# Loads, first stage and evictions of batch 1 moved in a Fourier filter with a snake feed-forward layer

## The chip, the cores and the metric

The kernel runs on one core of a Trainium2 chip. The metric is the device time of one execution in microseconds (us); the median of three runs counts.

## The reference

The input `x` has 8 batches of 3008 positions with 256 channels. Each batch is filtered in the frequency domain, and every position then goes through a feed-forward layer of width 2048 with the snake activation:

```python
X = np.fft.rfft(x, axis=1)
y = np.fft.irfft(X * (filt_r + 1j * filt_i)[None], n=3008, axis=1)
h = y.reshape(24064, 256) @ w_in            # w_in 256 x 2048
s = np.sin(alpha * h)
out = (h + s * s / (alpha + 1e-9)) @ w_out  # w_out 2048 x 256
```

## The kernel before

**The arithmetic.** The transform of 3008 = 47 x 64 points is done as matrix products in fp16. Each batch passes four stages: `first` (DFT over 47, 16 matmuls `pa` of 512 columns, each evicted as half precision into `t1_h`), `forward` (DFT over 64 with the twiddles in `d_t`, 12 pairs of matmuls `pb`), the product with the filter, `inverse` (12 pairs `pc` with `e_t`) and `last` (16 groups `pd`, evicted into `y`). Between `first` and `forward`, and between `inverse` and `last`, the data goes through DRAM to change its layout: SP stores `t1_h` into `d1` (L186), GpSimd's queue loads it back as `t2` (L193); SP stores `g` into `d2` (L239) and loads `t4` from it (L244). The filter is applied by `product` (L215, p = xf x real part) and `cross` (L221, L222: the halves of `xf` swapped by two SP copies `xs`, times `f_t[1]`, added to p). Both run on VectorE. Because the swap needs a sign, one half of `f_t[1]` is negated once, in two instructions of 64 x 3072 (`negate`, L602), before batch 1's cross products. Batch 0 goes another way, without DRAM, by VectorE transposes (L413) at the start of the kernel; it uses the filter without that sign.

**The feed-forward layer.** The 2048 x 256 hidden layer runs in chunks of 512 positions. `hidden(k, jb)` makes one of 16 tiles of a chunk: two matmuls into a `ph` buffer (L540), a cosine on ScalarE (L544), and `v = cos - 1 - ph` on VectorE (L545). `project` multiplies the `v` of the chunk before by `w_out` (groups of eight matmuls `po`, L557); ScalarE copies the result to `o` (L565), and SP stores it. `w_in` is scaled by alpha and `w_out` by -0.5/alpha on GpSimd (`weights_in`, L482, six pieces; `weights_out`, L514, three pieces of four blocks; the last four blocks on ScalarE, L512).

**Buffers.** PSUM has four `ph` buffers (`h`), two for `po` (`o`), and two (`f`) that all transform matmuls share. `evac` (L160, L162) empties an `f` buffer: every third call goes to VectorE, the others to ScalarE, unless the call names the engine.

**The order of the work.** Engines take their instructions in program order, and program order is written by hand. At the start stand batch 0's stages; then GpSimd gets the weight products and the loads of batch 1's `x`. The main loop counts steps: each makes two `hidden` tiles and one or two `project` groups (chunk 0 has only the tiles), and `slot(step)`, called twice a step, takes from a sorted list what is due. The list is filled by `put(time, function, ...)`; of the entries marked `pe`, one is taken per call, and more only when they are overdue by a step. For batch 1 `first` is due from 7.9, `load_t2` at 12.5, `negate` at 13 and 14, `forward` from 17.5, `cross` from 21.5, `inverse` from 23.5.

**Order of loads.** SP loads `w_in` in six pieces, then `w_out` in two. `after(ins, other)` makes a DMA wait for another to land: the first piece of `w_in` waits for the last quarter of the filter (`marks["filt", 1, 1]`), and each `x` load of batch 1 for the first half of `w_out`. The filter comes in quarters on GpSimd's queue, real and imaginary part of each half of `s`; `other_half` copies each quarter to the other 64 partitions.

Of the kernel before, what the change touches and what calls it, by code (L numbers as in the profile page):

```python
# [62 lines left out]
def kernel(  # L63
# [10 lines left out]
    nc = tc.nc  # L74
# [12 lines left out]
    def after(ins, other):  # L87

        tc.add_manual_dep(ins.ins, other.ins.name, mybir.DependencyInfo(
            mybir.DependencyClass.Sync, mybir.DependencyReason.DATA), reason="order of loads")  # L90
# [43 lines left out]
    f_t = [filt_t[:, k] for k in range(2)]  # L134

    marks = {}
# [20 lines left out]
    def evac(dst, src, on_act=None):  # L157
        flip[0] = (flip[0] + 1) % 3
        if flip[0] if on_act is None else on_act:
            marks["act"] = nc.scalar.copy(out=dst, in_=src)  # L160
        else:
            marks["dve"] = nc.vector.tensor_copy(out=dst, in_=src)  # L162

    class Spectral:
# [59 lines left out]
        def inverse(self, w):  # L224
            b = self.b
            pr = self.p.pop(w)
            if w % 3 == 0:
                self.g = gpool.tile([128, 6, C], FP16, name=f"g_{b}_{w}", tag="g")
            ps = fps.tile([128, 2, C], FP32, name=f"pc_{b}_{w}", tag="f")
            for i in range(2):  # L230
                for k, pt in enumerate(pr):
                    nc.tensor.matmul(out=ps[:, i, :], lhsT=e_t[:, 2 * w + i, :],  # L232
                                     rhs=pt[:, i, :], start=(k == 0), stop=(k == len(pr) - 1))
            i0 = 2 * (w % 3)
            evac(self.g[:, i0:i0 + 2, :], ps)
            if w % 3 == 2:
                for p in range(2):
                    a0 = p * NS + 6 * (w // 3)
                    nc.sync.dma_start(out=self.d2[a0:a0 + 6, :, :].rearrange("s n c -> n s c"),  # L239
                                      in_=self.g[64 * p:64 * p + 64, :, :])  # L240
# [46 lines left out]
    def spread_alpha(i):  # L287

        ps = hps.tile([128, 4, 128], FP32, name=f"al_bc_{i}", tag="h")
        for a in range(4):  # L290
            for k, part in enumerate(parts):
                nc.tensor.matmul(out=ps[:, a, :], lhsT=one[:, 4 * i + a:4 * i + a + 1].to_broadcast([128, 128]),
                                 rhs=part, start=(k == 0), stop=(k == 2))
        nc.scalar.copy(out=alpha[:, i // 2, 512 * (i % 2):512 * (i % 2) + 512], in_=ps.rearrange("p a b -> p (a b)"))

    for g in range(2):
        gs = slice(12 * g, 12 * g + 12)
        for k, filt in enumerate((filt_r, filt_i)):
            for q in range(2):
                if (g, k, q) == (0, 1, 1):  # L300
                    split_alpha()
                off, step = ((12 * g) * C, C) if q == 0 else ((N1 - 12 * g) * C, -C)
                marks["filt", g, k] = nc.gpsimd.dma_start(
                    out=f_t[k][64 * k + 32 * q:64 * k + 32 * q + 32, gs, :],
# [91 lines left out]
    for i in range(16):  # L396
        own, tag = (fps, "f") if i % 3 == 2 else (hps, "h")
        ps = own.tile([128, 512], FP32, name=f"pa_0_{i}", tag=tag)
# [64 lines left out]
    for g in range(6):  # L463
        own, tag = (t2pool, "t2") if g < 3 else (gpool, "g")
        j0 = 1024 * (g // 3) + 384 * (g % 3)
        js = slice(j0, j0 + (256 if g % 3 == 2 else 384))
        w_in32.append((js, own.tile([128, 2, js.stop - js.start], FP32, name=f"w_in_{g}", tag=tag)))
        ins = nc.sync.dma_start(out=w_in32[g][1], in_=w_in_v[:, :, js])
        if g == 0:
            after(ins, marks["filt", 1, 1])  # L470
    nc.sync.dma_start(out=wf_t, in_=wf_dram.ap())
    nc.sync.dma_start(out=wi_t, in_=wi_dram.ap())
    w_out32 = vpool.tile([128, 16, C], FP32, name="w_out32", tag="v")
    for jb in range(0, 16, 8):
        ins = nc.sync.dma_start(out=w_out32[:, jb:jb + 8],
                                in_=moe_w_out[128 * jb:128 * jb + 1024].rearrange("(b p) c -> p b c", p=128))
        marks.setdefault("w_out", ins)
    s1 = Spectral(1)
# [37 lines left out]

    spread_alpha(2)
    spread_alpha(3)
    for step in ([(weights_in, g) for g in range(6)] + [(s1.load_x, 0), (weights_out, 0), (s1.load_x, 1),
                 (weights_out, 4), (s1.load_x, 2), (weights_out, 8), (s1.load_x, 3)]):  # L520
        step[0](*step[1:])
    warm_pe(12)
    last_0(0, 4)
# [69 lines left out]
    def put(at, fn, *args, pe=False):  # L593
        pending.append((at, len(pending), pe, fn, args))
# [4 lines left out]
    def negate(i):  # L599

        gs = slice(12 * i, 12 * i + 12)
        nc.vector.tensor_scalar(out=f_t[1][0:64, gs, :], in0=f_t[1][0:64, gs, :],  # L602
                                scalar1=-1.0, scalar2=None, op0=ALU.mult)

    for i in range(2):
        put(13 + i, negate, i)
    for n0, n, at in ((6, 5, 1.5), (11, 4, 12.5), (15, 4, 14), (19, 4, 15.5), (23, 4, 17), (27, 5, 19)):
        put(at, last_0, n0, n, fps, "f", True)
    for b in range(1, B):
        s = s1 if b == 1 else Spectral(b)  # L610
        z = 48 * b
        if b > 1:
            for ch in range(4):
                put((22,27,32,37)[ch] if b == 2 else z - 92 + 7 * ch, s.load_x, ch)
        for i in range(16):
            put(7.9 + 0.3 * i if b == 1 else 36 + 0.66 * i if b == 2 else z - 67 + 0.66 * i, s.first, i, pe=True)
        for g in range(4):
            put(12.5 if b == 1 else max(z - 56, 46.5), s.load_t2, g)
        for u in range(12):
            inv = 23.5 + 1.25 * u if b == 1 else 59 + 2.1 * u if b == 2 else z - 40.8 + 2.3 * u  # L620
            fwd = inv - (6 if b == 1 else 6)
            put(fwd, s.forward, u, pe=True)
            put(fwd + (0.5 if b == 1 else 1.5), s.product, u)
            if s.fused:
                put(fwd + (4 if b == 1 else 4.5), s.cross, u)
            put(inv, s.inverse, u, pe=True)
        for ch in range(4):
            put(z - (9.5 if b == 1 and ch < 3 else (10.5, 10.5, 10.5, 3)[ch]), s.load_t4, ch)
        for u in range(16):
            put(z + (u - (5 if b == 1 else 6.5) if u < 4 else 2 * u - 9), s.last, u, pe=True)  # L630
# [15 lines left out]
    step = 0  # L646
# [43 lines left out]
```

## Time and profile before

| What | Value |
|---|---|
| Median of 3 runs (lowest, highest) | 789.85 us (789.4, 790.68) |
| Profiled execution, span from the first to the last instruction | 786.7 us |
| TensorE busy | 773.5 us |
| VectorE busy | 657.6 us |
| ScalarE busy | 616.5 us |
| GpSimd busy | 79.5 us |
| First hidden matmul starts | 36.79 us |
| First `pa` matmul of batch 1 starts | 47.63 us |
| Mean granted TensorE clock | 1.000 |

The profile is of one execution. PE is TensorE's matmuls, PEld its weight loads, DVE VectorE, ACT ScalarE, POOL GpSimd, SP SyncE, which here only issues DMAs. A row of a timeline gives start, duration, engine, source line, operation, tile written `<-` tile read, shape and count; in brackets stands the idle time before it and what ended that. Matmul rows overlap, since they are pipelined: what one costs is read from the distance between the starts of two.

### The profile page before, as it was taken

How to read it: one execution, taken by the hardware profiler on the slowest of the kernel's cores; microseconds unless marked ns; L12 is line 12 of the kernel's file. 1: busy time of each engine (PE TensorE's matmuls, PEld its weight loads, DVE VectorE, ACT ScalarE, POOL GpSimd, SP SyncE). 2: the span in 40 equal slices, each digit the busy share in tenths (PEclk: the TensorE clock that was granted, in tenths of full speed). 3: DMA queues.
4: the chain of work that ended last, by engine and by line, in shares of the span. 5: the costliest groups of instructions: out<-in, count | busy, mean ns of one | idle time of the engine just before them, and what ended most of it. 6: DMA issues, size and time to landing. Idle time of an engine off the chain costs nothing.

```text
span 786.7 us, 16619 instructions
## 1 busy us (share of the span) xinstructions
PE 773.5 (98%) x5799; PEld 535.0 (68%) x5799; DVE 657.6 (84%) x1172; ACT 616.5 (78%) x1208; POOL 79.5 (10%) x125
## 2 busy tenths in 40 slices
PE   8998999999999999999999999999999999999998
PEld 4756766666667766777666766777666776766666
DVE  7887997899878997799977998799987999777773
ACT  5797878888878887888877888788887887777674
POOL 6442000200020000200020000200002000000000
PEclk9999999999999999999999999999999999999999
DMA  9965568665473646554575454845556243421111
GB/s 213 258 131 157 113 145 223 153 123 133 134 198 84 134 99 195 143 120 110 120 200 128 103 106 139 224 87 113 129 155 181 61 99 81 117 62 28 41 41 54
DMA packets 87692, 100.99 MB, mean 128 GB/s; under 512 B 14488, under 2 KB 75944, under 8 KB 87608
## 3 DMA queue, kind: packets, MB, share of 16 engines
q1 hardware_dynamic: 78032, 73.73, 34.5%
q0 software_dynamic: 9360, 26.15, 17.7%
q8 instruction: 45, 0.74, 0.4%
q14 instruction: 39, 0.32, 0.1%
q10 hardware_dynamic: 216, 0.05, 0.0%
HBM read 55.72 MB, written 46.66 MB: 130 GB/s over the span
## 4 chain that ended last, share of the span: by engine, by line
PE 89%; DVE 5%; ACT 2%; DMA 2%; issue 1%; SPq 1%; ACTq 0%; DVEq 0%
PE po L557 39%; PE ph L540 38%; PE pa L181 3%; PE pd L254 2%; DVE v L545 2%; PE pb L201 2%; PE pc L232 2%; DMA xs<-xf 1%; ACT cos_all L544 1%; DMA al<-in_moe_alpha_dram 1%; PE warm L381 1%; PE pc L453 0%; SPq L585 0%; ACT t_h L160 0%; DVE filt_t L162 0%
## 5 line engine op out<-in xcount | busy, mean ns | idle before, releaser
L545 DVE SCALAR_TENSOR_TENSOR v<-cos_all,ph 128x512 f16<-128x512 f32 (+1 forms) x768 | 483.0, 672 | 108.1 <-ACT cos_all L544 104.8
L544 ACT ACTIVATE cos_all<-ph 128x512 f32<-128x512 f32 (+1 forms) x768 | 411.1, 592 | 93.9 <-PE ph L540 92.9
L540 PE MATMUL ph<-y,w 128*128 128x512 f16 (+1 forms) x1536 | 388.4, 374 | 1.7 <-DVE y L162 0.9
L557 PE MATMUL po<-w,v 128*128 128x256 f16 x3008 | 389.5, 272 | 0.0
L557 PEld LDWEIGHTS <-v 128*128 128x128 f16 x3008 | 288.3, 98 | 77.7 <-issue 1.4
L540 PEld LDWEIGHTS <-w 128*128 128x128 f16 x1536 | 147.9, 98 | 106.5 <-issue 6.1
L565 ACT COPY o<-po 128x512 f32<-128x512 f32 (+1 forms) x97 | 55.6, 574 | 20.2 <-PE po L557 12.9
L204 ACT CAST xf<-pb 128x512 f16<-128x512 f32 x84 | 50.0, 595 | 16.4 <-PE pb L201 12.7
L193 POOL DMA_DIRECT2D t<-d x56 | 36.4, 669 | 204.6 <-DMA out_dram<-o 99.8
L160 ACT CAST t_h<-pa 96x512 f16<-96x512 f32 x74 | 43.3, 585 | 10.6 <-PE pa L181 10.5
L141 POOL DMA_DIRECT2D x<-in_x_dram x32 | 17.1, 536 | 298.2 <-PE pc L232 171.2
L160 ACT CAST y<-pd 128x376 f16<-128x376 f32 (+1 forms) x82 | 39.5, 482 | 8.8 <-PE pd L254 5.3
L254 PEld LDWEIGHTS <-t_a 96*128 96x128 f16 x448 | 31.3, 97 | 18.7 <-issue 0.4
L181 PE MATMUL pa<-x,wf_t 94*96 94x512 f16 x112 | 42.3, 381 | 1.6 <-ACT t_h L160 1.3
L160 ACT CAST g<-pc 128x512 f16<-128x512 f32 x58 | 34.4, 593 | 8.0 <-PE pc L232 7.7
L222 DVE TENSOR_TENSOR p<-p,xs 128x512 f16<-128x512 f16 x84 | 35.7, 425 | 2.9
L254 PE MATMUL pd<-wi_t,t_a 96*128 96x94 f16 x448 | 37.1, 204 | 0.0
L221 DVE TENSOR_TENSOR xs<-xs,filt_t 128x512 f16<-128x512 f16 x84 | 35.2, 420 | 0.8 <-DMA xs<-xf 0.8
L215 DVE TENSOR_TENSOR p<-xf,filt_t 128x512 f16<-128x512 f16 x84 | 35.2, 419 | 0.0
L232 PE MATMUL pc<-p,e_t 128*128 128x256 f16 x168 | 32.1, 273 | 0.8 <-ACT xf L204 0.5
L201 PE MATMUL pb<-t,d_t 128*128 128x256 f16 x168 | 32.1, 272 | 0.2
L162 DVE CAST y<-pd 128x376 f16<-128x376 f32 (+2 forms) x46 | 24.9, 544 | 1.5 <-PE pd L343 1.0
(66 smaller groups left out, 264.4 us busy)
## 6 DMA issues: line engine op xcount, KB each, us to landing
x<-in_x_dram POOLq DMA_DIRECT2D x30, 376.0 KB, 4.9
d<-t_h SPq DMA_DIRECT2D x28, 384.0 KB
t<-d POOLq DMA_DIRECT2D x56, 192.0 KB, 4.6
xs<-xf SPq DMA_DIRECT2D x168, 64.0 KB
d<-g SPq DMA_DIRECT2D x56, 192.0 KB
t_a<-d SPq DMA_DIRECT2D x28, 384.0 KB
out_dram<-o SPq DMA_DIRECT2D x104, 80.0 KB
w_out<-in_moe_w_out_dram SPq DMA_DIRECT2D x2, 1024.0 KB
```

Of the source, the lines that this page charges most:

```text
L160: marks["act"] = nc.scalar.copy(out=dst, in_=src)
L181: marks["pe"] = nc.tensor.matmul(out=ps[0:NK, :], lhsT=wf_t, rhs=self.x[ch][:, 2 * j:2 * j + 2, :], start=True, stop=True)
L193: nc.gpsimd.dma_start(out=self.t2[g][64 * p:64 * p + 64, :, :], in_=self.d1[a0:a0 + 6, :, :].rearrange("s n c -> n s c"))
L201: nc.tensor.matmul(out=ps[:, i, :], lhsT=d_t[:, s, :], rhs=self.t2[s // 6][:, s % 6, :], start=True, stop=True)
L204: nc.scalar.copy(out=self.xf[u], in_=ps)
L232: nc.tensor.matmul(out=ps[:, i, :], lhsT=e_t[:, 2 * w + i, :], rhs=pt[:, i, :], start=(k == 0), stop=(k == len(pr) - 1))
L254: nc.tensor.matmul(out=psv[:, i, :], rhs=wi_t, start=True, stop=True, lhsT=t4_h[ch // 2][0:NK, n0 % 16 + i, cb * 128:cb * 128 + 128])
L540: nc.tensor.matmul(out=ps[:, 0:n], lhsT=w1[:, cb, jb * 128:jb * 128 + 128], rhs=y_cols[:, cb, c0:c0 + n], start=(cb == 0), stop=(cb == 1))
L544: nc.scalar.activation(out=cs[:, 0:n], in_=ps[:, 0:n], func=AFT.Sin, bias=float(np.pi / 2))
L545: marks["snake"] = nc.vector.scalar_tensor_tensor(out=v[k][:, jb, 0:n], in0=cs[:, 0:n], scalar=-1.0, in1=ps[:, 0:n], op0=ALU.add, op1=ALU. ...
L557: nc.tensor.matmul(out=pso[k][:, t % 2, :], lhsT=v[k][:, jb, 128 * t:128 * t + 128], rhs=w2[:, jb, :], start=(jb == 0), stop=(jb == 15))
L565: nc.scalar.copy(out=o[:, i0:t % 2 + 1, :], in_=pso[k][:, i0:t % 2 + 1, :])
```

## The change

Five edits, all about the time in which batch 1's transform gets going:

1. The load of `w_in` waits for the third quarter of the filter instead of the last.
2. On GpSimd the four `x` loads of batch 1 stand between the last three `w_in` products; the three `w_out` products follow all of them. Before, all six `w_in` products came first, and the `x` loads stood between the `w_out` products.
3. Batch 1's first stage is due from step 6.9 in steps of 0.35, instead of from 7.9 in steps of 0.3.
4. The evictions of batch 1's inverse stage all go to ScalarE; before, every third went to VectorE.
5. The two negations of the filter half run on GpSimd instead of VectorE, behind the `t2` loads in its queue.

```diff
@@ inverse
-            evac(self.g[:, i0:i0 + 2, :], ps)
+            evac(self.g[:, i0:i0 + 2, :], ps, True if b == 1 else None)
@@ loads of w_in
         if g == 0:
-            after(ins, marks["filt", 1, 1])
+            after(ins, marks["filt", 1, 0])
@@ GpSimd's weight products
-    for step in ([(weights_in, g) for g in range(6)] + [(s1.load_x, 0), (weights_out, 0), (s1.load_x, 1),
-                 (weights_out, 4), (s1.load_x, 2), (weights_out, 8), (s1.load_x, 3)]):
+    for step in ([(weights_in, g) for g in range(3)] + [(s1.load_x, 0), (weights_in, 3), (s1.load_x, 1),
+                 (weights_in, 4), (s1.load_x, 2), (weights_in, 5), (s1.load_x, 3)]
+                 + [(weights_out, jb) for jb in (0, 4, 8)]):
         step[0](*step[1:])
@@ negate
-        nc.vector.tensor_scalar(out=f_t[1][0:64, gs, :], in0=f_t[1][0:64, gs, :],
+        nc.gpsimd.tensor_scalar(out=f_t[1][0:64, gs, :], in0=f_t[1][0:64, gs, :],
                                 scalar1=-1.0, scalar2=None, op0=ALU.mult)
@@ the list of the main loop
-            put(7.9 + 0.3 * i if b == 1 else 36 + 0.66 * i if b == 2 else z - 67 + 0.66 * i, s.first, i, pe=True)
+            put(6.9 + 0.35 * i if b == 1 else 36 + 0.66 * i if b == 2 else z - 67 + 0.66 * i, s.first, i, pe=True)
```

## The prediction

> **What bounds the kernel now.** I read the page's busy row first, then busy time by stage, then the timelines of TensorE, VectorE, ScalarE and GpSimd through the stages that the diff touches.
>
> ```profile
> PE 773.5 (98%) x5799; PEld 535.0 (68%) x5799; DVE 657.6 (84%) x1172; ACT 616.5 (78%) x1208; POOL 79.5 (10%) x125
> 40.00:60.00 20.00, 18.61 (x104) 10.46 (x103) 17.06 (x29) 17.80 (x37) 7.93 (x8) 1.00 0.66 129
> 60.00:80.00 20.00, 17.90 (x149) 13.99 (x148) 15.10 (x26) 14.77 (x30) 5.22 (x8) 1.00 0.57 152
> 80.00:100.00 20.00, 20.00 (x147) 14.28 (x146) 19.54 (x41) 17.08 (x33) 1.09 (x2) 1.00 0.59 121
> 100.00:120.00 20.00, 19.12 (x126) 12.09 (x125) 18.76 (x37) 15.15 (x30) 1.03 (x2) 1.00 0.64 147
> 160.00:200.00 40.00, 39.95 (x299) 27.96 (x297) 37.84 (x74) 33.59 (x66) 1.03 (x2) 1.00 0.54 121
> ```
>
> The stage rows give busy us of PE, PEld, DVE, ACT, POOL, then clock, DMA share and GB/s. From 160 us on TensorE has no idle time: every microsecond won or lost before then moves the end by as much, and nothing later can win any. The stretch from 40 to 120 us, which fills the pipeline and runs batch 1's transform, is where TensorE still waits.
>
> ```profile
> 57.10 1.04 PE L557 MATMUL po<-w,v 128*128 128x256 f16 x8
> 58.25 0.38 PE L181 MATMUL pa<-x,wf_t 94*96 94x512 f16 x1
> 59.29 0.38 PE L181 MATMUL pa<-x,wf_t 94*96 94x512 f16 x1 [0.67 <-ACT t_h L160]
> 61.46 0.38 PE L181 MATMUL pa<-x,wf_t 94*96 94x512 f16 x1
> 62.51 0.38 PE L181 MATMUL pa<-x,wf_t 94*96 94x512 f16 x1 [0.67 <-ACT t_h L160]
> 66.56 0.20 PE L343 MATMUL pd<-wi_t,t_a 128*128 128x94 f16 x1 [0.34 <-ACT y L160]
> 68.69 0.38 PE L540 MATMUL ph<-y,w 128*128 128x512 f16 x1 [0.90 <-DVE y L162]
> ```
>
> Two `pa` matmuls in a row start 0.22 apart when nothing holds them; here they start 1.04 and 1.05 apart. Of the pairs 11/12 and 14/15 the second waits for ScalarE to empty the `f` buffer that the first has just filled.
>
> ```profile
> 65.58 0.95 DVE L602 TENSOR_SCALAR filt_t<-filt_t 64x3072 f16<-64x3072 f16 x1
> 66.45 0.54 DVE L162 CAST y<-pd 128x376 f16<-128x376 f32 x1
> 66.91 1.27 DVE L545 SCALAR_TENSOR_TENSOR v<-cos_all,ph 128x512 f16<-128x512 f32 x2
> 68.10 0.54 DVE L162 CAST y<-pd 128x376 f16<-128x376 f32 x1
> 75.87 0.42 DVE L215 TENSOR_TENSOR p<-xf,filt_t 128x512 f16<-128x512 f16 x1
> 46.73 2.06 ACT L544 ACTIVATE cos_all<-ph 128x512 f32<-128x512 f32 x4
> 48.64 0.60 ACT L160 CAST t_h<-pa 96x512 f16<-96x512 f32 x1
> 12.40 0.58 POOL L307 DMA_DIRECT2D e_t<-e_tbl  x1
> 17.40 0.99 POOL L307 DMA_DIRECT2D e_t<-e_tbl  x1 [0.43 <-DMA filt_t<-in_filt_r_dram]
> 67.10 5.22 POOL L193 DMA_DIRECT2D t<-d  x8 [19.14 <-DMA d<-t_h]
> ```
>
> The negations of L602 stand ahead of evictions that TensorE needs; ScalarE runs its cosines without a gap from 46.73 to 48.64; GpSimd issues batch 1's `t` loads from 67.10 to 72.32.
>
> **Part by part.** The profiled span is 786.7 us against a median of 789.85, so 3.1 us lie around the span. Gains and losses below are differences of the span, taken off the median.
>
> *w_in's load.* The third quarter's last piece was issued at 15.16; the shortest flight of that tile's loads is 7.9, so it lands at 23.0. SP now issues `w_in` then instead of at 25.47, 2.4 earlier. It overtakes the last quarter and `e_t`'s second half on the DMA engines. VectorE's copy of the last quarter at 25.66 waits 0.2 for that landing, and from there products and transposes run nearly unbroken to the first hidden matmul at 36.79, so any delay is paid in full. In the trace the last 512-byte filter packet starts at 24.2; `w_in`'s first packet came 1.06 after its issue, thus now at 24.1. Bounds 0 and 0.9 (the longest of those first `w_in` packets, 0.88, ahead of the landing's signal); no gain, since the filter itself comes no earlier. I take 0.2 lost, near the lower end, as the packets hardly overlap.
>
> *x loads between the products.* GpSimd's first three products end at 35.4 as before. Behind them the x load waits for `w_out`'s first half, which landed at 38.33 by the landings in the trace and now at about 36.0; queued behind that wait are products 3 to 5 (1.82, 1.82, 1.28) and three `w_out` products (1.91). With 0.56 for each x issue, products 3, 4, 5 end at 38.4, 40.8, 42.6; their first readers on TensorE run at 41.26, 43.06, 45.41. `w_out`'s last product ends at 48.9, its reader runs at 50.7. So nothing, covered by 1.8 us or more. If `w_out` lands no earlier, everything is 2.3 later and some 0.5 is lost. x lands 4 to 5 us after issue, long before use.
>
> *First stage from 6.9.* The order now has `pa` 0 and 1 ahead of chunk 1, and the evictions of 10 and 13 stand ahead of VectorE's next two tiles. TensorE waits of 0.82, 0.82 (the two pairs) and 0.28 (at 58.25) were 1.92 in all. New waits: ScalarE cannot evict `pa` 0 before 47.7, so `pa` 2 starts at 48.3; by then TensorE has done two `pa` (0.43) where before it had one and half a `po` group (0.67): 0.23 lost. Following the order with pitches 0.48 (ScalarE), 0.60 (VectorE), 0.87 (eight `po`), `pa` 11 and 13 still wait 0.1 and 0.25. Net 1.92-0.23-0.35 = 1.35 won; bounds 0.7 (one pair still waits 0.82 in full) and 1.9.
>
> *Negation to GpSimd, what VectorE gets.* Two instructions of 0.95 go. The waits at 66.56 and 68.69, by start pitch 0.51 and 1.06, don't both vanish: the `y` that TensorE wants at 68.69 follows a cosine that ends at 67.0, one tile (0.60) and its own 0.54, thus 68.15 at best. Won 0.5; bounds 0.2 and 1.57. Next late is that cosine.
>
> *Negation to GpSimd, what it costs.* It is queued behind the eight `t` issues, ending 9.8 after `pa` 15 starts (72.32-62.51). No row shows this operation there. Nearest is the one-input CAST, 186 ns for 16 elements and 280 for 128, which makes 2.75 for 3072; the two-input form (1272 for 512, 1815 for 768) would make 6.7. I take 2.75, as this too has one input. Cross products (L221) now wait for GpSimd, but the first comes at 81.96: covered. Not covered is the first L215, due 12.9 after `pa` 15 (75.87-62.51, less 0.5), while the second negation runs until 15.3. Do the engines hold each other up? The `e_t` issue at 17.40 took 0.99 instead of 0.58, ending 0.12 after VectorE's SBUF copy of 17.32 to 18.27: held. The `v` rows beside GpSimd's products keep their 0.61: not held, but they read PSUM. L215 reads two SBUF tiles, so I take it as held, 2.4. Behind it stand the next `v` tiles. TensorE has four `ph` buffers; a pair is wanted back 4.2 later and its chain takes 2.2, so 2.0 is covered. Lost 0.5; bounds 0 and 8.3 (below).
>
> The Trainium skill, page "SBUF — State Buffer", section "Who interferes with whom", speaks against this edit: a VectorE instruction with two SBUF inputs and a GpSimd instruction that reads SBUF exclude each other for the whole instruction. No row here has that pair; by the rule the hold stands as taken, without it the sum would be 0.5 better. Its "GPSIMD Engine Reference", section 3.1, gives 1.03 cycles per element for simple bodies and about 1.8 for a tight loop; at the latter, an estimate is 4.6 us per negation, and the sum would turn to a loss of 1.25.
>
> *Inverse evictions.* In 80 to 120 VectorE is busiest. TensorE's waits from 100.44 to 115.8 come to 2.03 by start pitch. Three `g` casts (92.77, 101.55, 109.53), 0.60 each, leave it: 1.8. ScalarE gets 3 x 0.48 where it was idle 0.60 (before 91.73) and 1.68 (before 104.88). The wait of 0.64 at 101.30 is for an `xf` behind an `xs` copy, which SP issues behind the `d` store of `g`; that store now waits for ScalarE and may go 1 us earlier, or not. I leave it out and take 1.2 of the other 1.39; bounds 0 and 2.0.
>
> Sum: -0.2+1.35+0.5-0.5+1.2 = 2.35 won: 787.5.
>
> **Rivals.** *Slower: GpSimd's negation stops VectorE.* With d us per negation the hold is 9.8+2d-12.9, the loss 2d-5.1 after cover, against 2.85 won elsewhere; it decides from d = 4.0. At 6.7: 8.3 lost, 5.4 slower net, 795.3. For it: GpSimd's two-input rows and the held issue. Against: its one-input rows. *No hold*: the `v` rows speak for it; 2.85 won, 787.0. *Nothing measurable*: the `xs` copies, not VectorE, pace 100 to 116 (for it: ScalarE's 3.0 us of waits on them), and the early `w_in` costs 0.9: 1.35+0.5-0.5-0.9 = 0.45 won, 789.4.
>
> **How the numbers follow.** Forecast 0.42, no hold 0.17, nothing 0.15, slower rival 0.26. The range starts at 785.7, where about half of each upper bound beyond the forecast comes true as well, and ends at 791.7, the slower rival with d = 4.9; beyond lie long negations. A measurement of this kernel tells about 0.2% (1.6 us) from nothing; a little of the forecast's own spread falls inside. Faster 0.57, same 0.17, slower 0.26.
>
> **What would show it.** Right: `pa` pairs without 0.67 gaps and `pa` 15 near 61.3; `ph` at 68.69 some 1.9 earlier; GpSimd TENSOR_SCALAR rows near 2.75 from about 71; one L215 that starts or ends late beside them; no `g` on VectorE from 90 to 112. Wrong: negations over 4 us, a TensorE gap of over 1 us near 75 to 80, the first hidden matmul later than 37.2, or a `po` group that waits for `w_out` near 50.

## The result, and the profile after

The changed kernel takes 794.68 us (793.97 to 796.93, four runs) against 790.02 for the kernel before in the same session: a ratio of 1.0071, 95% interval 1.0053 to 1.009. It is 0.7% slower, where 0.3% faster was forecast. The profiled execution spans 792.5 us, 5.8 more than that of before.

The windows by stage (busy us of PE, PEld, DVE, ACT, POOL, then clock, DMA share and GB/s) show at once where the time is:

```profile
40.00:60.00 20.00, 18.99 (x108) 10.87 (x107) 17.65 (x30) 18.39 (x38) 9.81 (x8) 1.00 0.59 121
60.00:80.00 20.00, 18.41 (x154) 14.39 (x153) 16.05 (x20) 14.91 (x30) 14.83 (x10) 1.00 0.61 159
80.00:100.00 20.00, 14.39 (x89) 9.53 (x89) 19.45 (x32) 11.30 (x22) 7.01 (x2) 0.83 0.31 66
100.00:120.00 20.00, 20.00 (x145) 13.93 (x143) 18.53 (x40) 17.80 (x36) 1.03 (x2) 1.00 0.76 163
160.00:200.00 40.00, 39.92 (x303) 28.00 (x301) 37.85 (x75) 32.88 (x65) 1.56 (x3) 1.00 0.55 116
```

The stretch from 80 to 100, in which TensorE had no idle time before, now has 14.39 us of work instead of 20.00, at a clock of 0.83. The timeline rows of GpSimd, VectorE and TensorE around it (start, duration, engine, line, operation; in brackets the idle time before it):

```profile
65.17 5.27 POOL L193 DMA_DIRECT2D t<-d  x8 [15.32 <-DMA d<-t_h]
70.41 15.99 POOL L603 TENSOR_SCALAR filt_t<-filt_t 64x3072 f16<-64x3072 f16 x2
...
72.90 0.68 DVE L546 SCALAR_TENSOR_TENSOR v<-cos_all,ph 128x512 f16<-128x512 f32 x1
73.49 3.54 DVE L215 TENSOR_TENSOR p<-xf,filt_t 128x512 f16<-128x512 f16 x1
76.95 1.27 DVE L546 SCALAR_TENSOR_TENSOR v<-cos_all,ph 128x512 f16<-128x512 f32 x2
78.15 6.81 DVE L215 TENSOR_TENSOR p<-xf,filt_t 128x512 f16<-128x512 f16 x1
84.88 1.27 DVE L546 SCALAR_TENSOR_TENSOR v<-cos_all,ph 128x512 f16<-128x512 f32 x2
...
86.64 0.41 DVE L215 TENSOR_TENSOR p<-xf,filt_t 128x512 f16<-128x512 f16 x1
...
77.68 1.19 PE L541 MATMUL ph<-y,w 128*128 128x512 f16 x4 [0.54 <-DVE v L546]
...
85.61 1.87 PE L541 MATMUL ph<-y,w 128*128 128x512 f16 x4 [5.65 <-DVE v L546]
```

The chain reads upwards from the last row: TensorE waits 5.65 us for a `ph` buffer that VectorE's `v` has to free; `v` stands behind an L215 of 6.81 us, where one beside nothing takes 0.41 or 0.42; and that L215 runs while GpSimd negates, for 8.0 us an instruction. The first L215 comes free near the end of the first negation, and after two `v` the next is stopped by the second negation, so the hold comes in two parts: 3.54 and 6.81, less 0.42 each, 3.12 and 6.39. The list of waits for 72 to 92 puts the same on one line (waiter, its releaser: us in total, times, longest):

```profile
PE ph L541 <- DVE v L546: 6.2, 2, 5.6
```

By start pitch TensorE lost 0.71 and 5.81, 6.52 together. The shorter windows show what came on top:

```profile
82.00:85.00 3.00, 0.00 (x0) 0.00 (x0) 3.00 (x2) 0.00 (x0) 3.00 (x1) 0.69 0.00 0
85.00:88.00 3.00, 2.39 (x8) 1.10 (x8) 3.00 (x6) 1.08 (x2) 1.40 (x1) 0.50 0.03 5
88.00:90.00 2.00, 2.00 (x10) 1.28 (x9) 1.97 (x5) 0.46 (x2) 0.00 (x0) 0.51 0.00 0
90.00:92.00 2.00, 2.00 (x16) 1.36 (x14) 1.62 (x4) 1.70 (x4) 0.61 (x1) 1.00 0.29 66
```

After the gap the matmuls ran at half clock. From 85.61 to 90.55 stand eight of 512 columns and ten of 256, which at pitches of 0.215 and 0.108 make 2.80 us; they took 4.94, so 2.1 more were lost. The stop cost 6.52 + 2.1 = 8.6 us.

The rest of the change shows too. The `pa` pairs wait 0.10 at most (the two of the row at 58.07 start 0.32 apart), the last `pa` comes at 60.57 instead of 62.51, the pair of waits at 66 and 68 has become one, and there is a new one far behind them:

```profile
48.00 0.38 PE L181 MATMUL pa<-x,wf_t 94*96 94x512 f16 x1 [0.42 <-ACT t_h L160]
...
58.07 0.70 PE L181 MATMUL pa<-x,wf_t 94*96 94x512 f16 x2
...
60.57 0.38 PE L181 MATMUL pa<-x,wf_t 94*96 94x512 f16 x1
...
121.31 0.38 PE L232 MATMUL pc<-p,e_t 128*128 128x256 f16 x2 [1.04 <-DVE t_h L162]
```

### The profile page after: what moved, and what is told of

Its sections match the earlier page's. It is cut to its first block, busy times and chain, and to the rows that moved or that the text cites. A ratio compares the mean times of both kernels' runs of the same rounds, so it can differ in the third digit from the quotient of the medians.

```text
span 792.5 us, 16619 instructions
## 1 busy us (share of the span) xinstructions
PE 774.0 (98%) x5799; PEld 535.9 (68%) x5799; DVE 664.1 (84%) x1167; ACT 618.0 (78%) x1211; POOL 95.9 (12%) x127
## 4 chain that ended last, share of the span: by engine, by line
PE 90%; DVE 4%; DMA 2%; ACT 2%; issue 1%; SPq 0%; ACTq 0%; DVEq 0%
PE po L558 39%; PE ph L541 38%; PE pa L181 3%; PE pd L254 2%; DVE v L546 2%; PE pc L232 2%; PE pb L201 2%; ACT cos_all L545 1%; DVE p L215 1%; PE pc L453 1%; DMA al<-in_moe_alpha_dram 1%; PE warm L381 1%; PE pb L431 1%; DMA t_a<-d 0%; SPq L586 0%
## 5 line engine op out<-in xcount | busy, mean ns | idle before, releaser
L566 ACT COPY o<-po 128x512 f32<-128x512 f32 (+1 forms) x97 | 55.6, 573 | 19.6 <-PE po L558 12.9
L215 DVE TENSOR_TENSOR p<-xf,filt_t 128x512 f16<-128x512 f16 x84 | 44.7, 532 | 0.0
L160 ACT CAST g<-pc 128x512 f16<-128x512 f32 x61 | 36.3, 595 | 8.9 <-PE pc L232 8.6
L222 DVE TENSOR_TENSOR p<-p,xs 128x512 f16<-128x512 f16 x84 | 35.7, 425 | 2.9
L221 DVE TENSOR_TENSOR xs<-xs,filt_t 128x512 f16<-128x512 f16 x84 | 35.2, 419 | 1.0 <-DMA xs<-xf 1.0
```

What stands on the lines that cost most here:

```text
L215: marks["prod", u] = nc.vector.tensor_tensor(out=pt, in0=self.xf[u], in1=f_t[k][:, 2 * u:2 * u + 2, :], op=ALU.mult)
L566: nc.scalar.copy(out=o[:, i0:t % 2 + 1, :], in_=pso[k][:, i0:t % 2 + 1, :])
```

## Experiments

My theory after the result: the whole loss is the hold of L215 by GpSimd's negations, which last 8.0 us instead of 2.75; the other edits win about what was said. The rivals: that the other edits lose as well; that any long GpSimd instruction holds VectorE; and, for the last of the four rows above, that it is the `xs` copy and not a buffer that `pc` waits for. The three sessions timed the kernel before at 788.62, 788.56 and 788.32 us; a thousandth is 0.79 us.

**e1: the changed kernel with the negations back on VectorE.**

```diff
-        nc.gpsimd.tensor_scalar(out=f_t[1][0:64, gs, :], in0=f_t[1][0:64, gs, :],
+        nc.vector.tensor_scalar(out=f_t[1][0:64, gs, :], in0=f_t[1][0:64, gs, :],
```

> The changed kernel with its two negations back on VectorE, all else kept. Theory H (GpSimd's 8 us negations hold VectorE's L215, whose rows took 3.54 and 6.81 instead of 0.42): TensorE's gap of 5.8 us at 80 and the half clock behind it go, clock 1.00 throughout, and the four other edits show what they bring together: span 786.7 - 3 = 783.7, time 787.1 (786.0 to 788.3). Rival R (the moved loads or the early w_in cost the time, by transfers that come late): time stays above 792.

Measured: 786.67 us, ratio 0.9978 (0.9969 to 0.9987). The other edits together win 1.7 us. No L215 is held and the clock stays at 1.00. Against the changed kernel's 1.0071, one engine's name is worth 0.93%, 7.3 us. But TensorE now waits 1.71 us in a place where before had 0.37 and 0.28, shown here by its own row:

```profile
113.00 0.38 PE L232 MATMUL pc<-p,e_t 128*128 128x256 f16 x2 [1.55 <-DVE t_h L162]
...
110.27 0.43 DVE L221 TENSOR_TENSOR xs<-xs,filt_t 128x512 f16<-128x512 f16 x1 [1.22 <-DMA xs<-xf]
...
112.27 0.68 DVE L162 CAST t_h<-pa 96x512 f16<-96x512 f32 x1
```

The last inverse pair of batch 1 takes an `f` buffer that a `pa` of batch 2 has filled. Two `pa` stand ahead of the pair, and by the count of `evac` the first goes to VectorE, the second to ScalarE. VectorE empties the first one's buffer at 112.27 (`t_h`), behind its last cross product, which waited until 110.27 for the `xs` copy.

**e2: before with the negations alone on GpSimd.** The same line the other way, in before.

> The kernel before with only its negations moved to GpSimd. Theory H: negation rows of 8 us behind the t loads (from about 72), two L215 rows of over 3 us, a TensorE gap of about 6 us near 82 with a half clock after it; 8 to 9 us slower than before, 798 to 799. Rival R: within 1 us of before.

Measured: 797.34 us, ratio 1.0116 (1.0102 to 1.013), 9.1 us lost. The rows are those of the changed kernel, 1.7 us later:

```profile
72.14 15.98 POOL L602 TENSOR_SCALAR filt_t<-filt_t 64x3072 f16<-64x3072 f16 x2
...
75.25 3.50 DVE L215 TENSOR_TENSOR p<-xf,filt_t 128x512 f16<-128x512 f16 x1
...
79.86 6.81 DVE L215 TENSOR_TENSOR p<-xf,filt_t 128x512 f16<-128x512 f16 x1
...
87.33 1.86 PE L540 MATMUL ph<-y,w 128*128 128x512 f16 x4 [5.65 <-DVE v L545]
```

One edit alone makes the loss; the others only hide part of it.

**e3: GpSimd negates before the `t` loads, long ahead of L215.**

```diff
-        put(13 + i, negate, i)
+        put(9 + i, negate, i)
```

> The changed kernel with GpSimd's negations queued ahead of the t loads (due at 9 and 10 instead of 13 and 14), so that they run from about 50 to 66 beside VectorE's v instructions, which read one SBUF tile and one PSUM tile, and end before the first L215. Theory H (only instructions with two SBUF inputs are held): v rows stay at 0.60 to 0.61 from start to start, L215 rows 0.42, time 787.1 (786.0 to 788.5; up to 1 us lost if the t loads start late). Rival S (GpSimd's work slows whatever VectorE does, as shared bandwidth would): v rows over 0.7, time above 790. Negation rows still near 8 us if their length is GpSimd's own, near 3 if it came from the contention.

Measured: 786.72 us, ratio 0.998 (0.9971 to 0.9989), as good as e1. The negations take as long as ever:

```profile
49.46 15.91 POOL L603 TENSOR_SCALAR filt_t<-filt_t 64x3072 f16<-64x3072 f16 x2
...
73.82 0.42 DVE L215 TENSOR_TENSOR p<-xf,filt_t 128x512 f16<-128x512 f16 x1
```

So their length alone does no harm; what counts is what they lie beside. Next to them run VectorE's `v` and `t_h` rows, which read at most one tile from SBUF, and these keep their 0.68 to 0.69 each. (The profiled execution, 788.37 us, was the slowest of e3's; its waits are not taken as typical.)

**e4: eight negations of 64x768 instead of two.**

```diff
-        gs = slice(12 * i, 12 * i + 12)
+        gs = slice(3 * i, 3 * i + 3)
...
-    for i in range(2):
-        put(13 + i, negate, i)
+    for i in range(8):
+        put(13 + 0.25 * i, negate, i)
```

> The changed kernel with GpSimd's negation cut into eight instructions of a quarter of the length, same place in its queue. Theory H (the port is held for one instruction at a time): negation rows of about 2.0, L215 rows of at most 2.4, several of them held, VectorE gets in between; TensorE loses 0 to 1.5 us, no half clock; 787 to 789. Rival S (shared bandwidth): the same total loss as in the changed kernel, 793 to 795.

Measured: 787.68 us, ratio 0.999 (0.9981 to 0.9999). GpSimd works a little longer than in the changed kernel, 16.96 us, beside the same VectorE rows, and the stop is gone:

```profile
70.12 16.96 POOL L603 TENSOR_SCALAR filt_t<-filt_t 64x768 f16<-64x768 f16 x8
...
72.26 2.19 POOL L603 TENSOR_SCALAR filt_t<-filt_t 64x768 f16<-64x768 f16 x1
...
82.75 2.16 POOL L603 TENSOR_SCALAR filt_t<-filt_t 64x768 f16<-64x768 f16 x1
...
73.19 0.62 DVE L215 TENSOR_TENSOR p<-xf,filt_t 128x512 f16<-128x512 f16 x1
...
74.93 0.99 DVE L215 TENSOR_TENSOR p<-xf,filt_t 128x512 f16<-128x512 f16 x1
...
83.32 0.98 DVE L221 TENSOR_TENSOR xs<-xs,filt_t 128x512 f16<-128x512 f16 x1
```

One instruction of 2.18 us holds VectorE for at most 0.57 us, which the four `ph` buffers cover: by start pitch TensorE waits 0.29 and 0.22 between 70 and 92, as in before (0.29 and 0.23). The length of the single GpSimd instruction made the loss, not the sum. The two single negations above are the ones that hold the first and the last row shown: each held row ends 0.6 us before its negation's row does. Of the twelve rows of L215, L221 and L222 that start beside negations, five are held; the other seven keep 0.41 to 0.43, so VectorE is not shut out for the whole of a negation's row. e4 is 0.9 us slower than e1, with intervals that overlap; in its profiled execution the late `pc` waits longer, 2.53 us.

**e11: what of GpSimd's work holds VectorE?** e1 with four memsets of 64x3008, which only write SBUF, where the negations stood on GpSimd.

```diff
+    def fill(cb):
+        nc.gpsimd.memset(y[0:64, cb, 1], 0.0)
+    for i in range(4):
+        put(13 + 0.25 * i, fill, i % 2)
```

> The changed kernel with the negations back on VectorE, and with four GpSimd memsets of 64x3008 fp16 added where the negations stood, on a part of `y` that is not in use then; nothing reads what they write. The memset rows of before (165 ns for 16 elements, 266 for 128) make some 2.5 us of each, an estimate. (a) VectorE's L215 is held by what GpSimd reads from SBUF: the memsets only write, L215 keeps 0.42 in every row beside them, and TensorE shows no wait over 1.2 us between 70 and 90. (b) Rival: any long GpSimd instruction on SBUF holds it: one or two L215 rows last 1.5 to 3 us, the hold and the memset ending within 1.5 us of each other.

Measured: one run, 786.33 us. The memsets stand in just the right place and hold nothing:

```profile
70.39 10.31 POOL L611 MEMSET y<- 64x3008 f16 x4
...
73.97 0.41 DVE L215 TENSOR_TENSOR p<-xf,filt_t 128x512 f16<-128x512 f16 x1
...
75.50 0.41 DVE L215 TENSOR_TENSOR p<-xf,filt_t 128x512 f16<-128x512 f16 x1
```

So a GpSimd instruction of 2.67 us that only writes does not hold L215, where one of 2.18 that reads and writes did. (The two memset rows give 2.9 us, not 2.5, for one of this length.) This is what the Trainium skill's "SBUF — State Buffer", section "Who interferes with whom", states: a VectorE instruction with two SBUF inputs is stopped by a GpSimd instruction that reads SBUF and not by one that only writes it. Row and rule agree, 0.41 here against 3.54 and 6.81 above. The rival that L215 waits for data is out: a wait for GpSimd's result stands in brackets, as in e12's `v` row below, and the held rows have none; L215 also reads the real part of `filt_t`, and the negations are of the imaginary one. But the memsets differ from the negations in the tile as well, `y` instead of `filt_t`, and no run has a GpSimd instruction that reads another tile beside L215. That it is the reading that counts is shown by e11 and the rule together, not by e11 alone.

**e5: before with the inverse evictions alone on ScalarE.**

```diff
-            evac(self.g[:, i0:i0 + 2, :], ps)
+            evac(self.g[:, i0:i0 + 2, :], ps, True if b == 1 else None)
```

> The kernel before with only batch 1's inverse evictions on ScalarE. The prediction put 1.2 us on this edit (0 to 2.0). Theory T (VectorE paces 100 to 116): the waits of 2.03 us there fall to about 0.8, 1.2 us faster. Rival W (they turn into one new wait: the last inverse pair needs an f buffer that VectorE empties behind the last cross product, which waits for its xs copy): the small waits go, one of 1.5 to 2.7 us stands before the last pc near 114, and the time is within 0.5 us of before; with a gap over 2 us also some us of half clock, up to 1.5 us slower.

Measured: 788.14 us, ratio 0.9995 (0.9986 to 1.0004): no difference to be told. TensorE's waits of 0.64, 0.37 and 0.28 between 100 and 116 are gone, and one of 1.59 has come, of the kind seen in e1:

```profile
114.38 0.38 PE L232 MATMUL pc<-p,e_t 128*128 128x256 f16 x2 [1.43 <-DVE t_h L162]
...
113.65 0.68 DVE L162 CAST t_h<-pa 96x512 f16<-96x512 f32 x1
```

The same three steps in before, `pc` and the evictions of the two `pa` ahead of it:

```profile
115.18 0.58 ACT L160 CAST t_h<-pa 96x512 f16<-96x512 f32 x1
...
115.82 0.38 PE L232 MATMUL pc<-p,e_t 128*128 128x256 f16 x2
...
115.90 0.68 DVE L162 CAST t_h<-pa 96x512 f16<-96x512 f32 x1
```

`evac` counts every call, also one that names its engine, so the edit moves no other eviction: batch 2's first `pa` goes to VectorE in both kernels and its second to ScalarE. What differs is the buffer that `pc` gets. In before it starts as ScalarE's eviction ends and before VectorE's begins, so it has the second `pa`'s buffer; in e5 it waits for VectorE, so it has the first one's. Why the pool hands out the other one, no run shows.

**e6: before with the first stage alone from 6.9.**

```diff
-            put(7.9 + 0.3 * i if b == 1 else 36 + 0.66 * i if b == 2 else z - 67 + 0.66 * i, s.first, i, pe=True)
+            put(6.9 + 0.35 * i if b == 1 else 36 + 0.66 * i if b == 2 else z - 67 + 0.66 * i, s.first, i, pe=True)
```

> The kernel before with only batch 1's first stage due from 6.9 in steps of 0.35; loads as before. The prediction put 1.35 us on this edit (0.7 to 1.9): pa 15 starts near 61.2 instead of 62.5, the pairs 1.04 apart are gone, one wait of 0.6 before pa 2 comes, 0.9 to 1.4 us faster. Rival: the x loads, which land later without the second edit, hold the earlier pa matmuls, so that nothing is won.

Measured: 787.06 us, ratio 0.9977 (0.9968 to 0.9986), 1.8 us won. The waits of 0.83, 0.84 and 0.28 went, one of 0.59 came, before the third `pa` and for ScalarE, whose wait the working had at 0.23.

**e8 and e9: is the late `pc` a matter of batch 2's early `pa`?** e8 is e1 with batch 2's first stage put later, e9 is e8 with VectorE's negations earlier.

```diff
-            put(6.9 + 0.35 * i if b == 1 else 36 + 0.66 * i if b == 2 else z - 67 + 0.66 * i, s.first, i, pe=True)
+            put(6.9 + 0.35 * i if b == 1 else 37.4 + 0.58 * i if b == 2 else z - 67 + 0.66 * i, s.first, i, pe=True)
```

> The changed kernel with the negations on VectorE and the first stage of batch 2 due from 37.4 in steps of 0.58 instead of 36 in steps of 0.66, so that no pa matmul of batch 2 stands ahead of batch 1's last inverse pair, and that pair's buffer is one that ScalarE empties. Theory W (the gap of 1.7 us at 111 is a buffer that VectorE empties behind its last cross product): gap under 0.5, some 1.2 us below the kernel with negations on VectorE alone, 785.4. Rival: the pair waits for its own operand, which comes from that cross product and its xs copy: gap stays over 1 us, time 786.7.

```diff
-        put(13 + i, negate, i)
+        put(10 + 1.4 * i, negate, i)
```

> As the run before in this call, and VectorE's negations due at 10 and 11.4 instead of 13 and 14, where VectorE waits for cosines 0.2 to 0.4 us at a time. Expected: the waits of 0.51 and 1.06 before the hidden matmul at 66.3 fall to one of about 1.0, as when GpSimd negates; 0.5 us below the run before, 784.9. Rival: each negation delays an eviction that the first stage needs, and the same 0.5 us is lost near 58.

Measured: 790.44 us, ratio 1.002 (1.0011 to 1.003), where 785.4 was expected, and 788.97, ratio 1.0006 (0.9996 to 1.0017), where 784.9 was. The wait before `pc` went, so batch 2's `pa` ahead of it is its cause; but in its place batch 2's forward stage now waits for its loads:

```profile
145.06 0.58 PE L201 MATMUL pb<-t,d_t 128*128 128x256 f16 x2 [3.33 <-DMA t<-d]
```

As a remedy it is worse than the wait. From e8 to e9 the two waits of 0.51 and 1.06 near 66 became one of 0.99, the 0.5 forecast for VectorE's relief; the times differ by 1.1 us, with intervals that overlap.

**e10: the best of it.** The changed kernel, VectorE's negations at 10 and 11.4, batch 2's first two evictions on ScalarE, so that the buffer is not emptied behind the cross product.

```diff
-            evac(t1_h[ch // 2][0:NK, r0 + 2 * j:r0 + 2 * j + 2, :], ps[0:NK, :])
+            evac(t1_h[ch // 2][0:NK, r0 + 2 * j:r0 + 2 * j + 2, :], ps[0:NK, :],
+                 True if self.b == 2 and i < 2 else None)
...
-        nc.gpsimd.tensor_scalar(out=f_t[1][0:64, gs, :], in0=f_t[1][0:64, gs, :],
+        nc.vector.tensor_scalar(out=f_t[1][0:64, gs, :], in0=f_t[1][0:64, gs, :],
...
-        put(13 + i, negate, i)
+        put(10 + 1.4 * i, negate, i)
```

> The changed kernel with the negations back on VectorE, but at steps 10 and 11.4, and with the evictions of batch 2's first two groups of `pa` on ScalarE. What each theory expects: (a) The wait before the last inverse pair of batch 1 (1.71 us before pc at 113.00 where the negations were put back alone) comes from the `f` buffer that VectorE empties behind its last cross product: with ScalarE as the one that empties it, the wait falls under 0.6, the small waits of 100 to 112 stay away, and the time is some 1.1 to 1.5 us below that kernel's 0.9978 of before, that is about 0.996 (785.2 to 785.6 against 788.6); the pair of 0.51 and 1.06 before ph near 66 falls to about 0.99 for 0.5 of it. (b) Rival: that pair waits for its own operand, the `xs` copy behind it: the wait stays over 1.2 whoever empties the buffer, and the ratio is 0.9972 or higher.

Measured: 784.29 us, ratio 0.9946 (0.9933 to 0.9958), 4.3 us faster than before and some 1.2% faster than the changed kernel (0.9946 over 1.0071). The late `pc` no longer waits, and the windows from 80 to 120 show TensorE without idle time:

```profile
80.00:100.00 20.00, 20.00 (x146) 14.10 (x145) 19.54 (x43) 18.20 (x36) 1.08 (x2) 1.00 0.65 135
100.00:120.00 20.00, 20.00 (x141) 13.87 (x140) 17.61 (x33) 17.21 (x35) 1.03 (x2) 1.00 0.78 177
```

The gain beats the 0.996 expected: the profiled executions put waits of 1.71, 0.58 and 0.29 of e1's away, 2.6 us, and the ratios differ by 0.0032, 2.5 us. It was the buffer, not the operand: VectorE's cross products still wait 1.0 us for an `xs` copy there.

**e12 and e13: the loads.** e12 is before with the two edits of the loads alone; e13 is e10 without them.

```diff
-            after(ins, marks["filt", 1, 1])
+            after(ins, marks["filt", 1, 0])
...
-    for step in ([(weights_in, g) for g in range(6)] + [(s1.load_x, 0), (weights_out, 0), (s1.load_x, 1),
-                 (weights_out, 4), (s1.load_x, 2), (weights_out, 8), (s1.load_x, 3)]):
+    for step in ([(weights_in, g) for g in range(3)] + [(s1.load_x, 0), (weights_in, 3), (s1.load_x, 1),
+                 (weights_in, 4), (s1.load_x, 2), (weights_in, 5), (s1.load_x, 3)]
+                 + [(weights_out, jb) for jb in (0, 4, 8)]):
```

> Before with only the two edits of the loads: w_in issued behind the third filter quarter, and batch 1's x loads between the products of w_in. (a) The prediction's terms: 0.2 lost (0 to 0.9) for the early w_in, nothing for the x loads: the first hidden matmul starts at 36.8 to 37.7 instead of 36.79, and the ratio is 1.0000 to 1.0012. (b) Rival, from the profile after, where the first hidden matmul started at 36.49: the early load costs nothing and wins 0.3 us: ratio 0.9993 to 1.0000.

> The kernel of the run before last but one (VectorE's negations at steps 10 and 11.4, batch 2's first two groups evicted by ScalarE) with the loads as before: w_in behind the last filter quarter, x of batch 1 between the products of w_out. (a) The loads are worth nothing: its ratio lies within 0.0008 of that kernel's. (b) Rival: with the first stage from 6.9, which asks for x earlier, the old loads come too late: pa 0, due about 1 us sooner, waits for x, TensorE shows a wait of over 0.5 us between 46 and 48 that the other kernel lacks, and the ratio is 0.001 or more higher.

Measured: e12 789.44 us, ratio 1.0012 (1.0003 to 1.0022), a loss of 0.9; e13 784.94, ratio 0.9954 (0.9941 to 0.9968), not to be told from e10's 0.9946. In e12 the first hidden matmul starts at 36.98, and there is a wait that no one had forecast:

```profile
44.13 5.59 POOL L514 TENSOR_TENSOR w<-w_out,rec_t 128x1024 f16<-128x1024 f32 x3
...
49.76 1.29 DVE L546 SCALAR_TENSOR_TENSOR v<-cos_all,ph 128x512 f16<-128x512 f32 x2 [0.94 <-POOL w L514]
...
51.70 0.38 PE L181 MATMUL pa<-x,wf_t 94*96 94x512 f16 x1 [0.47 <-DVE t_h L162]
```

`w_out32` lies in a buffer of the `v` pool. VectorE's first `v` of chunk 1 needs that buffer, so it waits for the last `w_out` product, which the moved `x` loads and `w_in` products have put 2.3 us later than in before. VectorE's delay reaches TensorE as 0.63 by start pitch. With the earlier first stage (e10) VectorE waits there too, 1.43, but TensorE does not.

## Why the prediction was wrong

The step that failed is the term "negation to GpSimd, what it costs", and in it the choice of d: "I take 2.75, as this too has one input". The chip took 8.0 us for 3072 elements, 2.6 ns each, above the one-input CAST's slope of 0.84 and above the two-input rows' 2.12, from which the upper bound of 6.7 came. Both ends were worked out from other operations, and the count of inputs was no ground to prefer the lower. The Trainium skill's "GPSIMD Engine Reference", section 3.1, from which the prediction drew an estimate of 4.6, does not agree with the trace either; the trace decides.

The mechanism was the slower rival's, with its place right: L215 stopped behind the `t` issues, `ph` buffers used up, from d = 4.0 on the deciding term. Its formula, a loss of 2d - 5.1, gives 10.9 at 8.0. Measured were 8.6, for two reasons it left out, with opposite signs: VectorE gets in between the two instructions, so the hold is 3.12 + 6.39 instead of 12.9 in one; and half clock behind the gap adds 2.1. That the measured 794.68 lies near this rival's 795.3 is luck: its d of 6.7 was 1.3 short, and the formula lost too much for its d. The range ended at 791.7, d = 4.9, although the text itself had 6.7 as possible at 795.3; a bound of the likeliest unknown was left out of the range.

The other terms, one by one:
- *First stage, 1.35 won (0.7 to 1.9).* e6 measured 1.8 (1.1 to 2.5). Right, and the waits gone are those of the working (1.95). Of the new ones `pa` 2's was 0.59 instead of 0.23, `pa` 13's 0.10 instead of 0.25, and `pa` 11 didn't wait.
- *Negation off VectorE, 0.5 won.* Right: the two waits of 1.57 became one of 0.99 wherever VectorE did not negate at that place (the changed kernel, e3, e4, e9, e10).
- *w_in, 0.2 lost, and the x loads, nothing.* e12 gives 0.9 lost (0.2 to 1.7) for both. "Covered by 1.8 us or more" looked at one reader of `w_out`'s products, TensorE, and not at the next owner of the buffer they read from. And the wait of 0.2 that the working gives VectorE's copy at 25.66 is that of the copy at 19.75, for the second quarter; at 25.66 the row has no wait, since VectorE is busy until 25.62. The start of the first hidden matmul decides nothing: among the kernels with the old loads it lies from 35.89 to 37.20, among those with the new ones from 36.02 to 36.98.
- *Inverse evictions, 1.2 won.* e5 measured 0.4 (0.3 lost to 1.1 won). The small waits went as forecast, the 0.64 that the working left out among them, but the last `pc` got a buffer that VectorE empties behind a cross product, and the new wait of 1.59 took the gain back. e10, where ScalarE empties the buffers of both `pa`, no longer has either.

Without the GpSimd term the sum was 0.5 higher for the hold and 0.5 lower for the relief, the same 2.35; e1, which is that kernel, measured 1.7 (1.0 to 2.4).

## What to carry to other kernels

Before work moves to an idle engine, find the duration of that very operation on it, or carry both ends of the bound into the range; then ask which instruction of the other engine shares a resource with it, and how long a single one of them holds it, since here eight short instructions added nothing to TensorE's waits where two long ones cost it 8.6 us. Where a pool of buffers is shared, a change of the engine that empties some can change which buffer a later matmul gets: look which eviction it now stands behind. And the end of a read frees a buffer for its next owner, who waits as a reader does.

## What the runs showed of the hardware

- GpSimd's TENSOR_SCALAR on fp16 took 8.0 us for 64x3072 and 2.18 for 64x768, about 2.6 to 2.8 ns per element of a partition; its memset of 64x3008 took 2.67.
- In the changed kernel the first negation's row ends at 78.47 and the L215 it held at 77.03; the second's at 86.40 and 84.96: 1.44 us before the row's end both times, and in e2 as well (78.75 and 80.19, 86.68 and 88.12). In e4, whose negations are a quarter as long, the five held rows end 0.6 us before. So the hold ends ahead of the row's end by a time that grows with the length of the instruction; a fixed lag of GpSimd's rows is not the reason. Whether the reading ends early or the rows run long, no run tells.
- TensorE's clock: behind the gap of 5.81 it was at half until 90; in the profiled execution of e3 a gap of 2.33 was followed by 0.56 and 0.58 over 114 to 118, in that of e4 one of 2.69 by 0.50 and 0.70, while behind 1.71 in e1 it stayed at 1.00.
